# Another order for the weight splits of a Strassen-Winograd expert layer

## The chip, the cores and the metric

The kernel runs on one core of one Trainium2 chip. The metric is the device time of one execution in microseconds (us). Engines are named as the profile names them: PE is TensorE, DVE is VectorE, ACT is ScalarE, POOL is GpSimd, SP is the queue from which this kernel issues its loads and stores.

## The reference, cut to what matters

Causal attention with a forgetting bias (4 batches, 8 heads, 576 positions, head size 64) gives an array x of 2304 x 512. It goes through a mixture of four dense experts:

```python
p = domain_probs / (domain_probs.sum(-1, keepdims=True) + 1e-09)
out = np.zeros((N, D), dtype=np.float32)
for e in range(E):                       # E = 4, D = 512, F = 1024
    h = np.maximum(x @ w1[e], 0.0)
    out += p[:, e:e + 1] * (h @ w2[e])
```

The change lies in the experts' part alone, in the way in which w2 is made ready.

## The kernel before, in words

Every float32 operand of a matmul is split into a high and a low half in a rounded format (suffixes h and l: `w1h`, `w1l`, `w2h`, `w2l`), and each product is taken as high x high, high x low and low x high. A split is two steps: `hi` (L371) writes the rounded copy, here always on ACT, and `sub` (L366, instruction on L367) takes the copy from the original, on DVE or POOL.

Up to about 418 us the kernel computes attention and expert 0, interleaved by a planner. Then comes the Strassen part: experts 1 to 3, each cut into two halves of its hidden columns (`HALVES`, six of them, n = 0 to 5), each half over three groups of 768 rows (`PAIRS`, g = 0 to 2). That makes 18 pieces of work. For one piece the first layer and the second layer are each a 2 x 2 block product done with seven products instead of eight. The first layer (`first_layer`, matmuls on L1044) takes its products in the order 1, 6, 5, 7, 2, 4, 3, twelve matmuls of 384 columns each. The second (`second_layer`, L1052) takes them in the order 4, 1, 2, 6, 5, 7, 3, eighteen matmuls of 256 columns each, six into each of three PSUM banks.

The six PSUM banks of `pb` and the two of `mo` are handed on as follows. First layer: products 1, 6, 7 and 4 add up in the pair `bA`, products 5 and 3 in `bB`, product 2 in `bC`. Between them ACT copies `bA` out (`keep`, L1082, two activations, called c11, c12, c22 and h21) and DVE adds `bB` or `bC` to such a copy (`plus`, L1086, two instructions, called c22, c11 and c12). Second layer: product 4 writes `lB`, which is both banks of `bC` and then the second bank of `bB`; product 1 writes `lA`, which is the two `mo` banks and the first of `bB`. DVE then adds the result to `acc` (`update`, L1145).

The loop runs the first layer of the next piece ahead of the second layer of the present one, so PE goes L1(0), L1(1), L2(0), L1(2), L2(1) and so on. Everything else is laid by hand into the gaps between products: behind each first-layer product o, `after(o)` issues the load of the next operand (SP), then the steps of the table `at` for o, and then steps of the list `side` (two of them in the very first piece, one in all others).

- The table steps make the second layer's activation operands. In most pieces the table is `REST = {1: "6 5", 6: "s3 7", 5: "3"}`: behind product 6 step s3 (a DVE instruction, L1056, that reads the copy c12) and then operand 7 (high half on ACT into `xg`, low half on POOL), behind product 5 operand 3 (high half on ACT into `hx`, which reads the result of s3, low half on POOL). In the very first piece the table is `START = {7: "4", 2: "1", 4: "s5 s7"}`.
- `side` holds, when a new half's w2 is due, the seven splits that `w_steps(2)` returns. In the first piece (n = 0) that is L1(0); for n = 1 to 5 it is the first layer of piece (n, 1), the last one before the second layer of (n, 0) needs the new w2. Each split is `hi` on ACT into `w2h` and `sub` on DVE into `w2l`. Two POOL sums (L849) hang on them: behind split 5, source 6 is made from source 5, in the same buffer `t`; behind split 2, source 4 is made from source 6 and the buffer `w2r` that split 2 has read. So split 6 waits for the first sum, and split 4 for the second.

Each engine works its own queue strictly in the order in which these functions issue; semaphores order the engines among themselves.

Of the kernel before, what the change touches and what calls it, by code (L numbers as in the profile page):

```python
# [277 lines left out]
def body(ctx, tc, qk, vp, s, dp, w1, w1s, w2, w2s, out):  # L278
# [87 lines left out]
    def sub(e, out, in0, in1):  # L366
        (nc.gpsimd if e == "POOL" else nc.vector).tensor_tensor(out=out, in0=in0, in1=in1, op=ALU.subtract)  # L367
# [10 lines left out]
    def hi(e, out, in_):  # L378
        if e == "ACT":
            nc.scalar.activation(out, in_, AF.Copy)  # L380
        elif e == "POOL":
            nc.gpsimd.tensor_scalar(out, in_, 1.0, 1.0, op0=ALU.mult, op1=ALU.mult)
        else:
            nc.vector.tensor_copy(out, in_)
# [76 lines left out]
    for j, (h, ms) in enumerate(VISITS):  # L461
        base = 1000.0 * (j + 1)
        b, hh = divmod(h, NH)
        o = 64 * (hh % 2)
# [34 lines left out]
        else:  # L499
            if pq:  # L500
                qk_ready = [ld, ldc]
            else:
# [6 lines left out]
                def f(e, j=j, h=h, ext=ext):  # L509
                    nc.sync.dma_start(out=tok["KK", j][0:64, :, 0:ext].bitcast(F32), in_=AB(j)[64:128, 0:1, 0:ext].bitcast(F32).to_broadcast([64, 2, ext]))  # L510
                    nc.sync.dma_start(out=tok["KK", j][64:128, 0, 0:ext].bitcast(F32), in_=AB(j)[64:128, 1, 0:ext].bitcast(F32))
                    nc.sync.dma_start(out=tok["KK", j][64:68, 1, 0:ext].bitcast(F32), in_=ced[h, 2:6, 0:ext])
# [250 lines left out]
    for gi, tiles in enumerate(GROUPS0):  # L763
# [4 lines left out]
        else:  # L768
# [9 lines left out]
            at = max(i for i, x in enumerate(prog) if x[0] == "l1e") + 1  # L778
# [50 lines left out]
    def temp():  # L829
        return tpool.tile([P, 2, TG], F32, tag="t", name="t")  # L830
# [9 lines left out]
    def load_operand(g, o):  # L840
        t = x_tile()
        if o in BASE:
            load_block(t, g, *BASE[o])
        else:
            nc.sync.dma_start(out=flat4(t), in_=xsv[g, SUMS[o]])
        return t

    def add(e, out, in0, in1, op):
        (nc.gpsimd if e == "POOL" else nc.vector).tensor_tensor(out=out, in0=in0, in1=in1, op=op)  # L849
# [69 lines left out]
    def w_steps(which, begin=False):  # L919

        b = stage.pop(which)
        neg = which == 2
        part = w1_part if which == 1 else w2_part
        src = {1: b[0, 0], 2: b[1, 0], 3: b[1, 1], 7: b[0, 1], 4: b[1, 0]}

        def sums():
            if begin:
                src[5], src[6], src[4] = (t.rearrange("p a b -> p (a b)") for t in (spool.tile([P, 1, 512], F32, tag="t2", name="t2"), temp(), temp()))
                src[5], src[6], src[4] = (t[:, 0:512] for t in (src[5], src[6], src[4]))
                add("POOL", src[5], b[0, 1], b[0, 0], ALU.subtract)  # L930
                add("POOL", src[7], b[1, 1], b[0, 1], ALU.subtract)
                add("POOL", src[6], b[1, 1], src[5], ALU.subtract)
                add("POOL", src[4], b[1, 0], src[6], ALU.subtract)
                return
            src[5] = src[6] = spool.tile([P, 1, 512], F32, tag="t2", name="t2")[:, 0]
            add("POOL", src[5], b[0, 1], b[0, 0], ALU.subtract)
            add("POOL", src[7], b[1, 1], b[0, 1], ALU.subtract)

        def split(o, e):
            hi("ACT", part(o, 0), src[o])  # L940
            sub(e, part(o, 1), src[o], part(o, 0).bitcast(F32))
            if begin:
                pass
            elif o == 5 and neg:
                add("POOL", src[6], src[5], b[1, 1], ALU.subtract)
            elif o == 5:
                add("POOL", src[6], b[1, 1], src[5], ALU.subtract)
            if o == 2 and not begin:
                add("POOL", src[4], src[4], src[6], ALU.add if neg else ALU.subtract)

        return [sums] + [lambda o=o, e=e: split(o, e) for o, e in (
            tuple((o, "DVE") for o in PRODUCTS) if begin else
            ((5, "POOL"), (1, "POOL"), (2, "POOL"), (6, "POOL"), (4, "POOL"), (7, "DVE"), (3, "DVE")) if which == 1 else
            ((5, "DVE"), (2, "DVE"), (1, "DVE"), (7, "DVE"), (6, "DVE"), (4, "DVE"), (3, "DVE")))]

    pmoe = ctx.enter_context(tc.tile_pool(name="psm", bufs=1, space=PSUM))
    pb = [pmoe.tile([P, 512], F32, name=f"pb{i}") for i in range(6)]
# [20 lines left out]
    def w1_sums():  # L978
        w1_first.extend(w_steps(1, True))
        w1_first.pop(0)()  # L980
# [58 lines left out]
    def product(o, x, ts, start):  # L1039
        wv = [w1_part(o, l).rearrange("p (k f) -> p k f", k=2) for l in range(2)]  # L1040
        for u in range(2):
            for k in range(2):
                for n, (wl, xl_) in enumerate(((0, 0), (0, 1), (1, 0))):
                    nc.tensor.matmul(ts[u][:, 0:TG], wv[wl][:, k, 128 * u:128 * u + 128], x[:, xl_, k, :],  # L1044
                                     start=start and k == 0 and n == 0, stop=k == 1 and n == 2, skip_group_check=not start)
# [18 lines left out]
    side = []  # L1064

    def first_layer(w_i, at, tmp):

        nxt = work[w_i + 1] if w_i + 1 < len(work) else None

        def after(o):  # L1070
            if nxt is not None:
                xt[o] = load_operand(nxt[1], o)
            for f in at.get(o, ()):
                f()
            for _ in range(1 if w_i else 2):
                if side:
                    side.pop(0)()

        def keep(name, ts, f=AF.Copy):
            tmp[name] = temp()  # L1080
            for u in range(2):
                nc.scalar.activation(tmp[name][:, u], ts[u][:, 0:TG], f)  # L1082

        def plus(name, ts):
            for u in range(2):
                nc.vector.tensor_tensor(out=tmp[name][:, u], in0=ts[u][:, 0:TG], in1=tmp[name][:, u], op=ALU.add)  # L1086

        product(1, xt[1], bA, True)
        keep("c11", bA)
        after(1)  # L1090
        product(6, xt[6], bA, False)
        keep("c12", bA)
        after(6)
        product(5, xt[5], bB, True)
        after(5)
        product(7, xt[7], bA, False)
        keep("c22", bA)
        plus("c22", bB)
        after(7)
        product(2, xt[2], bC, True)  # L1100
        plus("c11", bC)
        after(2)
        product(4, xt[4], bA, False)
        keep("h21", bA, AF.Relu)
        after(4)
        product(3, xt[3], bB, False)
        plus("c12", bB)
        after(3)
# [26 lines left out]
    def plan(steps, table):  # L1135
        return {o: [steps[x] for x in names.split()] for o, names in table.items()}

    def second_layer(n, g, at):
# [44 lines left out]
        after(3)  # L1183

    side.extend(w_steps(2))
    tmp = {}
    steps = operands(tmp)
    first_layer(0, plan(steps, START), tmp)
    for w_i, (n, g) in enumerate(work):
        more = n + 1 < len(HALVES)  # L1190
        if w_i + 1 < len(work):
            if g == 0 and more:
                stage_w1(*HALVES[n + 1])
            if g == 1 and more:
                w1_next = w_steps(1)
                side.append(w1_next.pop(0))
                stage_w2(*HALVES[n + 1])
            if g == 0 and n:
                side.extend(w2_next)
            tmp = {}  # L1200
            at = plan(steps, REST if w_i else FIRST)
            steps = operands(tmp, w_i + 2 == len(work))
            if w_i + 2 == len(work):
                at.update(plan(steps, LAST))
            first_layer(w_i + 1, at, tmp)
            while side:
                side.pop(0)()
        if g == 1 and more:
            side.extend(w1_next)
        if g == 2 and more:  # L1210
            w2_next = w_steps(2)
            side.append(w2_next.pop(0))
        second_layer(n, g, plan(steps, EARLY if w_i + 2 < len(work) else ALL if w_i + 2 == len(work) else {}))
        while side:
            side.pop(0)()
# [29 lines left out]
```

## Time and profile before

| | us |
|---|---|
| timed runs | 971.43, 969.35, 965.13; median 969.35 |
| the profiled execution, its own time | 966.64 |
| its span, first to last instruction | 964.9 |
| PE busy within the span | 944.0 (98%) |
| mean granted TensorE clock, as a share of full speed | 0.989 |

The profile records one execution. Its span is 1.7 us shorter than the time of the same execution, which is what lies around the first and the last instruction. A timeline row gives the start, the duration, engine, line, operation, the tile written and the tiles read, and in brackets the idle time of the engine ahead of it with what ended it; an "x2" row is two instructions back to back, and its duration covers both. An instruction's record begins when it leaves its engine's queue, so a wait for a resource inside the engine lengthens the record and is not shown as idle time.

### The profile page before, as it was taken

What the parts mean: (1) busy time and instruction counts of PE and PEld (TensorE: products, weight loads), DVE (VectorE), ACT (ScalarE), POOL (GpSimd) and SP (SyncE); (2) the same over time, 40 slices, a digit from 0 to 9 for tenths busy, and PEclk for the clock granted to TensorE, in tenths of its full rate; (3) what the DMA queues carried; (4) which work ended last, traced back from release to release, by engine and by line L of the source; (5) the groups of instructions that cost most, each with busy time, mean ns of one, the idle gap of its engine ahead of it and who ended that gap; (6) DMA issues with size and microseconds to landing.
All of it is one profiled execution on the core that took longest, in us unless ns stands there. A gap on an engine that the chain in (4) does not pass through costs nothing.

```text
span 964.9 us, 18367 instructions
## 1 busy us (share of the span) xinstructions
PE 944.0 (98%) x6346; PEld 891.5 (92%) x6346; DVE 734.5 (76%) x1825; ACT 446.7 (46%) x1144; POOL 450.0 (47%) x505
## 2 busy tenths in 40 slices
PE   9989999999999999999999999999999999999998
PEld 6668889898898999999999999999999999999998
DVE  5879889889886222257688967997797979688976
ACT  4658787777775211244343344423343425343341
POOL 4456555655541389522381265317343624481222
PEclk7989999999999999999999999999999999999999
DMA  5857766757642596759645666555865468644613
GB/s 144 223 148 195 207 187 194 212 168 211 172 138 92 190 336 242 267 170 373 218 147 200 219 229 221 190 179 187 273 231 168 156 221 273 224 146 152 217 34 115
DMA packets 125975, 189.75 MB, mean 197 GB/s; under 512 B 10478, under 2 KB 102154, under 8 KB 125882
## 3 DMA queue, kind: packets, MB, share of 16 engines
q1 hardware_dynamic: 125882, 188.57, 61.0%
q8 instruction: 51, 0.84, 0.3%
q14 instruction: 42, 0.34, 0.1%
HBM read 144.73 MB, written 29.54 MB: 181 GB/s over the span
## 4 chain that ended last, share of the span: by engine, by line
PE 80%; DVE 11%; ACT 2%; DMA 2%; issue 2%; POOL 2%; DVEq 0%; SPq 0%; ACTq 0%; POOLq 0%
PE pb L1052 20%; PE pb L1044 19%; PE mo L1052 8%; PE mo L759 6%; PE mo L746 5%; PE T L599 5%; DVE w2l L367 4%; PE pv L658 4%; PE pb L746 4%; PE pb L759 3%; PE S L551 3%; PE S L545 2%; DMA x<-x_d 1%; DVE t L1086 1%; DVE a L562 1%
## 5 line engine op out<-in xcount | busy, mean ns | idle before, releaser
L1044 PE MATMUL pb<-x,w1h 128*128 128x384 f32 x1008 | 255.9, 334 | 0.5 <-ACT t L1082 0.5
L1044 PEld LDWEIGHTS pb<-x,w1h 128*128 128x128 f32 x1008 | 181.2, 188 | 0.9 <-ACT t L1082 0.8
L1044 PE MATMUL pb<-x,w1l 128*128 128x384 f32 x504 | 168.4, 334 | 0.0
L367 POOL TENSOR_TENSOR hT_r<-t,hT_r 128x768 fp32r<-128x768 f32 x18 | 33.9, 1885 | 273.8 <-ACT hT_r L380 177.4
L1082 ACT ACTIVATE t<-pb 128x384 f32<-128x384 f32 x144 | 67.0, 487 | 169.4 <-PE pb L1044 160.2
L1145 DVE SCALAR_TENSOR_TENSOR acc<-pb,prob,acc 128x256 f32<-128x256 f32 x288 | 126.2, 474 | 9.4 <-PE pb L1052 9.2
L375 POOL TENSOR_SCALAR a<-a,sm 64x64 f32<-64x64 f32 (+4 forms) x147 | 92.0, 630 | 67.2 <-DVE sm L578 39.6
L1052 PE MATMUL pb<-w2h,hT_r 128*128 128x256 f32 x720 | 115.7, 283 | 0.1
L570 ACT ACTIVATE a<-a,mx 64x64 f32<-64x64 f32 (+4 forms) x160 | 89.6, 562 | 26.9 <-DVE mx L562 16.5
L1052 PEld LDWEIGHTS pb<-w2h,hT_r 128*128 128x128 f32 x720 | 100.0, 191 | 0.5 <-DVE t L1086 0.3
L1059 ACT ACTIVATE hT_r<-t 128x768 fp32r<-128x768 f32 x54 | 45.7, 846 | 108.1 <-PE pb L1052 104.5
L1044 PEld LDWEIGHTS pb<-x,w1l 128*128 128x128 f32 x504 | 94.6, 188 | 0.0
L1086 DVE TENSOR_TENSOR t<-pb,t 128x384 f32<-128x384 f32 x108 | 56.2, 550 | 50.3 <-PE pb L1044 35.1
L1056 DVE SCALAR_TENSOR_TENSOR t<-t 128x768 f32<-128x768 f32 x72 | 88.0, 1223 | 2.2 <-ACT t L1082 2.1
L746 PE MATMUL mo<-xg,w1h 128*128 128x256 f32 (+1 forms) x344 | 80.5, 308 | 1.0 <-DVE xg L367 1.0
L599 PE MATMUL T<-idn,a 128*128 128x128 f32 x473 | 74.9, 281 | 6.7 <-POOL a L375 3.6
L380 ACT ACTIVATE aTh<-T 128x256 fp32r<-128x256 f32 (+2 forms) x278 | 65.6, 308 | 28.3 <-PE T L599 23.9
L1052 PE MATMUL pb<-w2l,hT_r 128*128 128x256 f32 x360 | 73.0, 284 | 5.1 <-DVE w2l L367 5.1
L635 DVE TENSOR_TENSOR aTl<-T,aTh 128x64 fp32r<-128x64 f32 (+3 forms) x247 | 72.6, 334 | 6.3 <-ACT aTh L380 5.2
L599 PEld LDWEIGHTS T<-idn,a 128*128 128x128 f32 x473 | 55.0, 143 | 21.1 <-issue 7.1
L562 DVE CUSTOM_DVE_ANT_0 a<-S,mask 128x192 f32<-128x192 f32 (+4 forms) x151 | 61.9, 419 | 3.9 <-PE S L545 1.9
L1145 DVE SCALAR_TENSOR_TENSOR acc<-mo,prob,acc 128x256 f32<-128x256 f32 x144 | 62.7, 474 | 1.6 <-PE mo L1052 1.6
(160 smaller groups left out, 2101.7 us busy)
## 6 DMA issues: line engine op xcount, KB each, us to landing
x<-xs_d SPq DMA_DIRECT2D x68, 768.0 KB
x<-x_d SPq DMA_DIRECT2D x55, 768.0 KB
xs_d<-x SPq DMA_DIRECT2D x12, 768.0 KB
raw<-in_qk_dram SPq DMA_DIRECT2D x24, 288.0 KB
KK<-AB_r SPq DMA_DIRECT2D x24, 288.0 KB
x_d<-xh SPq DMA_DIRECT2D x12, 576.0 KB
w1r<-in_w1s_dram SPq DMA_DIRECT2D x6, 1024.0 KB
w2r<-in_w2s_dram SPq DMA_DIRECT2D x6, 1024.0 KB
```

The source lines that it names most:

```text
L367: (nc.gpsimd if e == "POOL" else nc.vector).tensor_tensor(out=out, in0=in0, in1=in1, op=ALU.subtract)
L375: (nc.gpsimd if e == "POOL" else nc.vector).tensor_scalar(out, in_, scale, 1.0 if bias is None else bias, op0=ALU.mult, op1=ALU.mult if bi ...
L562: nc.vector.tensor_tensor_reduce(out=z[0:n, j0:j1], in0=tok["S", (c, pi)][0:n, 0:j1 - j0], in1=mask[0:n, 448 - a + j0:448 - a + j1], scale ...
L570: nc.scalar.activation(z[0:n, 0:bb], z[0:n, 0:bb], AF.Exp, bias=tok["mx", c][0:n, k:k + 1], scale=-1.0, accum_out=tok["sm", c][0:n])
L599: nc.tensor.transpose(t[:, 128 * k:128 * k + 128], z[:, 128 * x:128 * x + 128], idn)
L635: nc.vector.tensor_tensor(out=dst, in0=src, in1=h_.bitcast(F32), op=ALU.subtract)
L746: nc.tensor.matmul(t[:, 0:w], wl[q][:, dc, o:o + P], xgt[:, l, dc, 0:w], start=(u == 0), stop=(u == 3 * KD - 1))
L759: nc.tensor.matmul(t, ht[:, fc, 128 * ti:128 * ti + 128], wl[fc // 2][:, fc % 2, :], start=(u == 0), stop=(u == 3 * KF - 1))
L1044: nc.tensor.matmul(ts[u][:, 0:TG], wv[wl][:, k, 128 * u:128 * u + 128], x[:, xl_, k, :], start=start and k == 0 and n == 0, stop=k == 1 an ...
L1052: nc.tensor.matmul(ts[t][:, 0:256], h_part(o, hl_)[:, k, 128 * t:128 * t + 128], wv[wl][:, k, :], start=start and k == 0 and n == 0, stop= ...
L1056: (nc.gpsimd if e == "POOL" else nc.vector).scalar_tensor_tensor(out=out, in0=in0, scalar=0.0, in1=in1, op0=ALU.max, op1=op)
L1145: nc.vector.scalar_tensor_tensor(out=a_, in0=ts[t][:, 0:256], scalar=prob[:, tt, e:e + 1], in1=a_, op0=ALU.mult, op1=ALU.add)
```

## The change

Two edits. The order in which `w_steps(2)` hands out the seven splits of w2 goes from 5, 2, 1, 7, 6, 4, 3 to 5, 2, 6, 4, 1, 7, 3. And behind first-layer product 6 the side steps are issued ahead of the table's steps; behind all other products they stay behind them.

```diff
             ((5, "POOL"), (1, "POOL"), (2, "POOL"), (6, "POOL"), (4, "POOL"), (7, "DVE"), (3, "DVE")) if which == 1 else
-            ((5, "DVE"), (2, "DVE"), (1, "DVE"), (7, "DVE"), (6, "DVE"), (4, "DVE"), (3, "DVE")))]
+            ((5, "DVE"), (2, "DVE"), (6, "DVE"), (4, "DVE"), (1, "DVE"), (7, "DVE"), (3, "DVE")))]
...
         def after(o):
             if nxt is not None:
                 xt[o] = load_operand(nxt[1], o)
-            for f in at.get(o, ()):
+            steps_ = at.get(o, ())
+            splits = [side.pop(0) for _ in range(1 if w_i else 2) if side]
+            for f in (*splits, *steps_) if o == 6 else (*steps_, *splits):
                 f()
-            for _ in range(1 if w_i else 2):
-                if side:
-                    side.pop(0)()
```

The splits of w1 and the steps of the second layer are handed out as before.

## Rows read from the trace of the kernel before

**Rows 1.** The page, part 1: busy time, share of the span, instructions

```profile
PE 944.0 (98%) x6346; PEld 891.5 (92%) x6346; DVE 734.5 (76%) x1825; ACT 446.7 (46%) x1144; POOL 450.0 (47%) x505
```

**Rows 2.** PE's waits over the span, the longest sum: us in total, times, longest

```profile
PE pb L1052 <- DVE w2l L367: 5.1, 5, 1.0
```

**Rows 3.** Stretches, one piece each: length, busy PE, PEld, DVE, ACT, POOL, clock

```profile
493.26:522.93 29.67, 29.67 (x211) 29.67 (x211) 24.00 (x44) 9.18 (x15) 9.57 (x6) 1.00 0.65 221
522.93:553.88 30.95, 29.94 (x212) 29.73 (x211) 28.74 (x47) 12.70 (x22) 10.04 (x5) 1.00 0.64 214
```

**Rows 4.** The chain that ended last: one first layer without waits (start, us)

```profile
553.88 14.56 PE pb L1044 x84
```

**Rows 5.** Timeline of PE, 537.2 to 540.9: the second layer's first product

```profile
537.34 0.63 PE L1052 MATMUL pb<-w2h,hT_r 128*128 128x256 f32 x4
538.98 0.50 PE L1052 MATMUL pb<-w2l,hT_r 128*128 128x256 f32 x2 [1.01 <-DVE w2l L367]
539.32 0.64 PE L1052 MATMUL pb<-w2h,hT_r 128*128 128x256 f32 x4
...
540.04 0.64 PE L1052 MATMUL pb<-w2h,hT_r 128*128 128x256 f32 x4
```

**Rows 6.** Timeline of DVE, 529 to 540, ahead of the same second layer

```profile
529.46 0.94 DVE L1056 SCALAR_TENSOR_TENSOR t<-t 128x768 f32<-128x768 f32 x1
530.33 4.04 DVE L367 TENSOR_TENSOR w2l<-w2r,w2h 128x512 fp32r<-128x512 f32 x2
...
535.22 0.85 DVE L367 TENSOR_TENSOR w2l<-w2r,w2h 128x512 fp32r<-128x512 f32 x1
535.99 1.01 DVE L1086 TENSOR_TENSOR t<-pb,t 128x384 f32<-128x384 f32 x2
536.92 1.40 DVE L367 TENSOR_TENSOR w2l<-t,w2h 128x512 fp32r<-128x512 f32 x1
538.25 0.68 DVE L367 TENSOR_TENSOR w2l<-w2r,w2h 128x512 fp32r<-128x512 f32 x1
538.85 1.01 DVE L1086 TENSOR_TENSOR t<-pb,t 128x384 f32<-128x384 f32 x2
```

**Rows 7.** Timeline of ACT, 528 to 537

```profile
528.17 0.86 ACT L380 ACTIVATE xg<-t 128x768 fp32r<-128x768 f32 x1
...
530.43 0.85 ACT L380 ACTIVATE hx<-t 128x768 fp32r<-128x768 f32 x1 [0.89 <-DVE t L1056]
...
531.71 0.85 ACT L1082 ACTIVATE t<-pb 128x384 f32<-128x384 f32 x2
...
535.84 1.15 ACT L380 ACTIVATE w2h<-w2r 128x512 fp32r<-128x512 f32 x2
```

**Rows 8.** Timeline of POOL, 529 to 538

```profile
529.61 1.95 POOL L849 TENSOR_TENSOR t<-t,w2r 128x512 f32<-128x512 f32 x1 [0.63 <-DVE w2l L367]
531.52 2.29 POOL L367 TENSOR_TENSOR xg<-t,xg 128x768 fp32r<-128x768 f32 x1
533.77 1.75 POOL L849 TENSOR_TENSOR w2r<-w2r,t 128x512 f32<-128x512 f32 x1
535.48 2.29 POOL L367 TENSOR_TENSOR hx<-t,hx 128x768 fp32r<-128x768 f32 x1
```

**Rows 9.** Timelines of DVE and of POOL around 442

```profile
441.52 2.60 DVE L1056 SCALAR_TENSOR_TENSOR t<-t 128x768 f32<-128x768 f32 x1
441.42 1.88 POOL L367 TENSOR_TENSOR hT_r<-t,hT_r 128x768 fp32r<-128x768 f32 x1 [15.18 <-ACT hT_r L380]
```

**Rows 10.** Timelines of POOL, DVE, ACT and PE in the first piece, 424 to 434

```profile
424.63 1.61 POOL L849 TENSOR_TENSOR w2r<-w2r,t 128x512 f32<-128x512 f32 x1 [0.85 <-DVE w2l L367]
427.31 1.01 DVE L1086 TENSOR_TENSOR t<-pb,t 128x384 f32<-128x384 f32 x2
433.11 0.85 ACT L1082 ACTIVATE t<-pb 128x384 f32<-128x384 f32 x2
433.64 0.62 PE L1044 MATMUL pb<-x,w1h 128*128 128x384 f32 x2 [0.52 <-ACT t L1082]
```

## The prediction

> **What bounds the kernel now.** I read the busy times first. PE is busy for 944.0 of 964.9 us [rows 1], so only PE's gaps can be won back, and whatever makes a new gap is paid in full. Next came PE's waits. In the Strassen part there are five waits for `w2l`, 5.1 us together and the longest 1.0, so all about equal [rows 2], and one of 0.52 us for the copy `t` in the first piece [rows 10]. The stretches then tell where the five lie: a piece without a wait lasts 29.67 us, the piece in which a new w2 is split lasts 30.95 [rows 3], so each wait costs 1.28 us, a little more than its idle time (the first matmuls behind a wait run slower: six that take 0.72 us elsewhere took 1.98 around the wait [rows 5]). As the five are equal, one piece worked out in detail holds for all. The ceiling of the change is therefore 5 x 1.28 = 6.4 us, with 0.8 more if the wait of the first piece went.
>
> In the timelines of this piece PE reaches the first `w2l` matmul of product 4 at 537.8 and gets it at 538.98, right behind split 4 on DVE, which ran from 538.25 to 538.93 [rows 5, 6]. The question is whether DVE's queue is merely in a bad order or simply late. Two things say late. Behind split 4 stands `plus` c12, 538.85 to 539.86 [rows 6], and it frees the bank that PE's third tile wants at 540.04 [rows 5]: with split 4 out of the way PE would find this bank ready only 0.1 us before today's time. And DVE's records are stretched: a split that takes 0.68 us at 538.25 takes 1.40 at 536.92, and two take 4.04 at 530.33 [rows 6].
>
> **What stretches them.** The ends line up with POOL's. Split 6 ends at 538.32, 0.55 behind POOL's end at 537.77; the pair ends at 534.37, 0.56 behind POOL's end at 533.81 [rows 6, 8]. The other way round POOL's first sum, begun at 529.61 while s3 was running, ends at 531.56, 1.16 behind the end of s3 at 530.40 [rows 6, 8]. Step s3's form waits too: at 441.52 it lasted 2.60 instead of 0.94 and ended 0.82 behind POOL [rows 6, 9]. `plus`, which reads one operand from PSUM, took 1.01 for two beside POOL's step of 535.48 (the pair at 535.99) and 1.01 without it (538.85) [rows 6, 8]. So a DVE and a POOL instruction that each read two SBUF tiles run one after the other, and when both queues are full they take turns. I use these figures: DVE split 0.68 alone, 0.55 behind POOL; s3 0.82 behind POOL; POOL's 512-column sum 1.16 behind DVE, its 768-column step 1.88 alone and 1.70 behind DVE (537.77 less the 536.07 at which the split of 535.22 ended) [rows 6, 8, 9].
>
> The Trainium skill (SBUF — State Buffer, "Who interferes with whom") says that issue order decides which of the two blocks for a whole instruction; the rows above agree. It makes the order of issue the thing to replay, and by it alone a reordering at equal work could come out either way.
>
> **The change, step by step, in the piece at 522.77.** It adds and removes no instruction and no DMA; SP's loads are issued ahead of both kinds of step, as before. Seven splits still stand on DVE, six of them ahead of `plus` c12. What changes is who meets whom, so I write the queues out anew from 529.46, the point at which split 5 has just ended and `after(6)` begins.
>
> 1. DVE now begins with split 2: 529.46 to 530.14. POOL's first sum, released at 529.61, follows it: to 530.14 + 1.16 = 531.30 (was 531.56).
> 2. s3 is now behind split 2 and meets that sum: it waits to 531.30 and ends at 532.12 (was 530.40). 1.7 us lost.
> 3. POOL's second sum, now ahead of operand 7, ends at 532.12 + 1.15 = 533.27 (was 535.52). This is what the change does for split 4.
> 4. ACT stands at operand 3's high half, which reads s3: 532.15 to 533.00 (was 530.43 [rows 7]). Behind it in ACT's queue are the high half of split 6 (0.62, half of 1.15 for two [rows 7]), to 533.52, and `keep` c22, whose two copies now end at 533.9 and 534.3 (was 531.71 to 532.56 [rows 7]).
> 5. PE: a product takes 14.56 / 7 = 2.08 us [rows 4], so with the second layer at 537.34 product 4 was due at 533.18. It adds into the bank that `keep` c22 reads, and now waits to 533.96: 0.78 idle, about 0.9 with the slow first matmuls. A new wait.
> 6. DVE's split 6 is ready at 533.55, but POOL has taken the turn at 533.27 with operand 7 and holds it to 535.15. Split 6 ends at 535.70, `plus` c22 at 536.6. POOL's operand 3 ends at 535.70 + 1.70 = 537.40, split 4 at 537.95, `plus` c11 at 538.9, split 1 at 539.5, split 7 at 540.1, `plus` c12 at 541.0 (was 539.86).
> 7. PE, 0.9 late, starts the second layer at 538.3 to 538.4. Split 4 is there (537.95), so the old wait is gone; but the third tile's bank comes free at 541.0 instead of 539.86, and PE begins it at 541.05 and runs its first matmuls 0.1 slower. Against 540.04 that is 1.1 us later.
>
> The same replay with the old order gives split 4 at 538.9 and the third tile at 540.1, as in the trace. The net is +1.1 us in each of five pieces, +5.5. Bounds: DVE could end no later than before, with PE then waiting for `plus` c12 at 539.9 (-0.1 a piece); at the other end one more 768-column step of POOL could fall in front of `plus` c12, of which half again is likely to be hidden (+1.9 a piece). I take 1.1, since 1.16, 0.55, 0.82 and 1.70 each come from rows with the same two instructions.
>
> **The first piece.** Here two splits stand behind each product; the new order puts 2 and 6 behind product 6, 4 and 1 behind product 5. Split 4's high half must wait for POOL's second sum, which ended at 426.24 [rows 10], and ACT has `keep` c22 behind it. So ACT: 426.3, two high halves (1.15 [rows 7]) to 427.4, first copy at 427.9; `plus` c22 starts at 428.2, not at 427.31 [rows 10]. Everything behind it on DVE and ACT is a closed chain up to `keep` h21 at 433.11, which releases PE at 433.64 [rows 10]: this chain, and so PE, slips by 0.86. PE's product 4 (due near 428.8, two products before 433) still finds its bank free. Bounds 0 and 1.2; I take 0.9.
>
> **The sum.** 5 x 1.1 + 0.9 = 6.4 us, on the profiled execution's 966.64: 973.0. That execution is 2.7 below the median of the three runs; all four together have their middle at 968.0 (halfway between 966.64 and 969.35). I put the change on that: 968.0 + 6.4 = 974.4 us, slower by 0.7%.
>
> **The rivals.**
> - *Faster: the wait simply goes.* Split 4 is ready 1 us earlier in step 6, and the wait for `w2l` is the only one that the profile names. It decides if DVE, too, gets through `plus` c12 at least 1.3 us sooner, so that all of 539.86 moves below 538.7. Price: -6.4, 961.6 us. Against it: `plus` c12 has as many splits ahead as before, and the turns with POOL are the same in number. The Trainium skill (Perfetto Trace Analysis, "Optimization Strategy") advises to find what PE's gap waits for and make that start sooner, which would give this time; the row of `plus` c12, 0.2 us ahead of PE [rows 5, 6], speaks against it here. Chance 0.10.
> - *No change: another wait takes its place at the same spot.* If DVE catches up in step 6 (split 6 taking its turn ahead of operand 7; 0.28 us decide), `plus` c12 ends near where it did: five times -0.1 to +0.4, and 0 to 0.9 in the first piece, 968 to 971. Chance 0.17.
> - *Worse:* the late `plus` c22 also delays product 3's bank, and an extra step of POOL falls ahead of `plus` c12: five times 1.9 and 1.2, 979 us. Chance 0.08.
>
> **How the numbers follow.** The forecast has 0.65. Its own range is 0.7 to 1.5 a piece and 0 to 1.2 in the first piece, 971.5 to 976.7, and with the 3 us by which the runs of before lie on either side of their middle 969 to 980. The range to hold the time 8 times in 10 takes in the no-change case and most of the worse one: 965 to 981. A measurement of this kernel can tell about 1% from no change, 9.7 us. The forecast and the no-change case lie within it, the faster rival too, unless the runs help it (0.02 over 1%); the worse case and the upper end of the forecast pass it with 0.12.
>
> **What would show it.** In the changed kernel PE's waits should hold no `w2l` any more, but five of about 0.8 us for `t` of ACT (product 4) and five of about 1.0 for `t` of DVE (third tile), and the first piece's 0.5 should have become 1.4; the piece of 30.95 should last 32.1. s3 should run for 2.0 us in a split piece. If the piece is shorter than 30.95, or s3 ends ahead of POOL's first sum, steps 2 to 7 are wrong.

## The result, and the profile after

The changed kernel takes 975.76 us (median of six runs, 973.75 to 979.28); the kernel before has 968.78 over six, the three runs of the table above among them. The ratio is 1.0083 with a 95% interval of 1.0054 to 1.0112: slower, by a little under 1%. The forecast was 974.4 us, slower by 0.7%.

Where the time went is read from stretches. This view of the changed kernel has one piece of work per row: length, busy time of PE, weight loads, DVE, ACT, POOL, clock.

```profile
499.49:529.16 29.67, 29.67 (x212) 29.67 (x211) 24.02 (x44) 9.19 (x15) 9.74 (x6) 1.00 0.65 221
529.16:561.13 31.97, 30.55 (x213) 29.62 (x211) 28.36 (x46) 12.69 (x22) 9.49 (x5) 1.00 0.62 207
```

A piece without splits is what it was, 29.67. A piece in which w2 is split went from 30.95 [rows 3] to 31.97, with PE idle for 1.42 us of it. The waits of PE over the whole span (us, times, longest) name two holders; five waits of each lie in the split pieces, and the sixth of the first row in the first piece:

```profile
PE pb L1044 <- ACT t L1081: 4.4, 6, 1.4
PE pb L1052 <- DVE t L1085: 4.2, 5, 0.8
```

The entry for `w2l` [rows 2] is gone; line numbers are one lower than before. The timeline of PE places the two in the split piece that began at 529.16:

```profile
540.32 0.62 PE L1044 MATMUL pb<-x,w1h 128*128 128x384 f32 x2 [0.58 <-ACT t L1081]
547.35 0.74 PE L1052 MATMUL pb<-w2h,hT_r 128*128 128x256 f32 x4 [0.84 <-DVE t L1085]
```

The first is product 4 of the first layer, waiting for the copy c22. The second is the third tile of the second layer's product 4, waiting for the addition c12. This piece began 6.39 us later on the clock than the one at 522.77, so 547.35 stands for 540.96 there, against 540.04 [rows 5]: 0.9 later. The timeline of DVE shows why; it answers to [rows 6]:

```profile
535.85 0.68 DVE L367 TENSOR_TENSOR w2l<-w2r,w2h 128x512 fp32r<-128x512 f32 x1
536.45 2.04 DVE L1056 SCALAR_TENSOR_TENSOR t<-t 128x768 f32<-128x768 f32 x1
539.92 2.05 DVE L367 TENSOR_TENSOR w2l<-t,w2h 128x512 fp32r<-128x512 f32 x1 [1.43 <-ACT w2h L380]
...
542.83 1.40 DVE L367 TENSOR_TENSOR w2l<-w2r,w2h 128x512 fp32r<-128x512 f32 x1
...
546.29 1.01 DVE L1085 TENSOR_TENSOR t<-pb,t 128x384 f32<-128x384 f32 x2
```

Split 2 runs alone in 0.68. Step s3 behind it takes 2.04 instead of 0.94, DVE then stands idle for 1.43 until ACT has the high half of split 6, and that split takes 2.05. The partners are in the timelines of POOL and of ACT ([rows 8] and [rows 7] before):

```profile
536.00 1.67 POOL L849 TENSOR_TENSOR t<-t,w2r 128x512 f32<-128x512 f32 x1 [0.63 <-DVE w2l L367]
537.75 1.89 POOL L849 TENSOR_TENSOR w2r<-w2r,t 128x512 f32<-128x512 f32 x1
539.60 1.82 POOL L367 TENSOR_TENSOR xg<-t,xg 128x768 fp32r<-128x768 f32 x1
541.38 2.31 POOL L367 TENSOR_TENSOR hx<-t,hx 128x768 fp32r<-128x768 f32 x1
```

```profile
538.52 0.85 ACT L380 ACTIVATE hx<-t 128x768 fp32r<-128x768 f32 x1 [2.58 <-DVE t L1056]
539.27 0.62 ACT L380 ACTIVATE w2h<-t 128x512 fp32r<-128x512 f32 x1
539.79 0.85 ACT L1081 ACTIVATE t<-pb 128x384 f32<-128x384 f32 x2
```

Step s3 ends at 538.49, 0.81 behind POOL's first sum (537.67); split 6 ends at 541.97, 0.55 behind operand 7 (541.42). ACT waits 2.58 for s3 with the high half of operand 3, and behind it in ACT's queue stand split 6 and the copy c22.

Five split pieces of 31.97 to 31.99 instead of 30.95 to 30.97 make 5.1 us. The first two pieces together take 45.97 instead of 45.06, 0.9 more; there the wait for the copy h21 grew from 0.52 [rows 10] to 1.44. From the start of the Strassen part to the end of the span that is 552.50 us instead of 546.50, and these 6.0 us are all that the change does. The profiled execution itself took 978.13, 11.5 more than the one before; the other 5.5 lie ahead of the first changed instruction, where both kernels issue the same work (last section).

### The profile page after: what moved, and what is told of

Read it like the earlier page. It is cut to its first block, busy times and chain, and to the rows that moved or that the text cites. A ratio compares the mean times of both kernels' runs of the same rounds, so it can differ in the third digit from the quotient of the medians.

```text
span 976.4 us, 18372 instructions
## 1 busy us (share of the span) xinstructions
PE 952.1 (98%) x6346; PEld 894.7 (92%) x6346; DVE 730.7 (75%) x1825; ACT 447.3 (46%) x1144; POOL 446.2 (46%) x505
## 4 chain that ended last, share of the span: by engine, by line
PE 75%; DVE 12%; DMA 4%; ACT 3%; issue 3%; POOL 1%; SPq 0%; DVEq 0%; ACTq 0%; POOLq 0%
PE pb L1044 19%; PE pb L1052 19%; PE mo L1052 8%; PE mo L759 6%; PE mo L746 4%; PE T L599 4%; PE pb L746 3%; PE pb L759 3%; PE pv L658 3%; DVE w2l L367 3%; PE S L551 3%; DVE t L1085 2%; DVE aTl L635 1%; DVE a L562 1%; DMA x<-x_d 1%
## 5 line engine op out<-in xcount | busy, mean ns | idle before, releaser
L1056 DVE SCALAR_TENSOR_TENSOR t<-t 128x768 f32<-128x768 f32 x72 | 93.5, 1298 | 2.2 <-ACT t L1081 2.1
L551 PE MATMUL S<-KK,AB_r 128*128 128x288 f32 (+9 forms) x288 | 62.1, 315 | 2.1 <-DVE mx L562 1.7
```

Of the source, the lines that this page charges most:

```text
L551: nc.tensor.matmul(t[:, 0:j1 - j0], AB(j)[0:k, x, a:a + P], tok["KK", j][0:k, x, j0:j1], start=(x == 0), stop=(x == 1))
L1056: (nc.gpsimd if e == "POOL" else nc.vector).scalar_tensor_tensor(out=out, in0=in0, scalar=0.0, in1=in1, op0=ALU.max, op1=op)
```

## The experiments

The lengths of like pieces repeat within 0.03 us inside one execution, so they tell theories apart that whole times could not. Theory A is the one of the prediction: DVE and POOL take turns, and POOL's steps are what makes DVE late. Theory B says that only the order in the queues matters and POOL runs beside DVE for nothing.

**The two edits one at a time.** First the order of the splits alone:

```diff
-            ((5, "DVE"), (2, "DVE"), (1, "DVE"), (7, "DVE"), (6, "DVE"), (4, "DVE"), (3, "DVE")))]
+            ((5, "DVE"), (2, "DVE"), (6, "DVE"), (4, "DVE"), (1, "DVE"), (7, "DVE"), (3, "DVE")))]
```

> The new order of the splits alone; behind product 6 the table's steps stay first. Measured by the length of a split piece (from the start of its first layer to that of the next one; 30.95 us before, 31.98 after) and of the first two pieces together (45.06 before, 45.97 after). Theory A, taking turns: DVE and POOL instructions that each read two SBUF tiles run one after the other, and the piece is as long as DVE's queue is late at its last additions. Split 4 must now wait on DVE for POOL's second sum, which still stands behind operand 7, so the additions c11 and c12 are as late as with the whole change: 32.1 us, with no wait at product 4, about 1.2 us for t of DVE ahead of the second layer and about 1.0 at its third bank. First two pieces 45.97. Theory B, queue order alone: what the change costs is that ACT's copy c22 stands behind operand 3 and s3; without the step ahead the copy is on time again, split 4 is early, and the piece is 29.7 us, at most 30.95.

Measured: 31.98 to 31.99 a split piece, first two pieces 45.99. PE's waits in one split piece, with the DVE row that bears on the first of them:

```profile
539.15 0.71 PE L1052 MATMUL pb<-w2h,hT_r 128*128 128x256 f32 x4 [0.98 <-ACT w2h L380]
541.66 0.74 PE L1052 MATMUL pb<-w2h,hT_r 128*128 128x256 f32 x4 [0.84 <-DVE t L1086]
```

```profile
538.46 1.01 DVE L1086 TENSOR_TENSOR t<-pb,t 128x384 f32<-128x384 f32 x2
```

The sums over the span:

```profile
PE pb L1052 <- DVE t L1086: 7.1, 8, 1.0
PE pb L1052 <- ACT w2h L380: 2.0, 2, 1.0
```

The length is that of A, and no wait stands at product 4. Ahead of the second layer PE waits 0.97 to 0.98 in each split piece. The view puts two of these five waits down to a high half on ACT and the other three to DVE's addition c11. In the piece shown ACT had made the high half of split 4 by 537.37, while the first of the two additions of c11 ended at 539.01, 0.14 ahead of PE's start; so here too the addition is what PE waits for, as A has it.

Then the step ahead alone, with the old order of the splits:

```diff
-            for f in at.get(o, ()):
+            steps_ = at.get(o, ())
+            splits = [side.pop(0) for _ in range(1 if w_i else 2) if side]
+            for f in (*splits, *steps_) if o == 6 else (*steps_, *splits):
                 f()
-            for _ in range(1 if w_i else 2):
-                if side:
-                    side.pop(0)()
```

> The other edit alone: the split ahead of the table's steps behind product 6, the splits in the old order. Theory A: split piece 32.1 us; PE waits 0.6 us for the copy t of ACT at product 4 and about 1.1 us for w2l in the second layer's first product, since DVE is as late as with the whole change. First two pieces 45.06 as before, because nothing stands in the table behind product 6 there. Theory B: the new wait at product 4 lies ahead of the old one for w2l, which shrinks by as much: 31 us.

Measured: 32.0 a split piece, first two pieces 45.07. The waits of a split piece:

```profile
531.48 0.61 PE L1044 MATMUL pb<-x,w1h 128*128 128x384 f32 x2 [0.58 <-ACT t L1081]
537.58 0.51 PE L1052 MATMUL pb<-w2l,hT_r 128*128 128x256 f32 x2 [0.86 <-DVE w2l L367]
```

Either edit by itself costs the five pieces as much as both together, about 1.0 us each, by different waits. The costs don't add, since both work through the same lateness of DVE: counted from the start of the piece and put on the time scale of the kernel before, the addition c12 ends at 540.93 with the order alone, at 540.91 with the step ahead alone and at 540.91 with both (539.86 before). And the 0.9 us of the first piece belong to the order alone.

**POOL's steps taken away.** The low halves of operands 7 and 3 are left out in the split pieces, once in the changed kernel and once in the kernel before:

```diff
     def operand(o, t, e):
         hi("ACT", h_part(o, 0), t)
+        if bare[0] and o in (7, 3):
+            return
         sub(e, h_part(o, 1), t, h_part(o, 0).bitcast(F32))
...
+            bare[0] = g == 0 and n > 0
             first_layer(w_i + 1, at, tmp)
+            bare[0] = False
```

> The changed kernel, in the five split pieces without POOL's low halves of operands 7 and 3 (left out: the second layer then takes stale low halves of these two). Theory A: DVE is held up by neither, split 6 ends at 1.4 us and the addition c12 at 1.9 us earlier than with the change; only the wait at product 4 stays, which comes from s3 behind POOL's first sum: 30.6 us a split piece, no wait for t of DVE. Theory B: POOL's steps run beside DVE and cost it nothing: 32.0 us.

> The kernel before with the same left out: in the five split pieces no low halves of operands 7 and 3 on POOL. Theory A: split 4 ends some 1.7 us earlier, at the time PE reaches product 4 of the second layer, and the wait for w2l goes: 29.67 us a split piece, the length of a piece without splits. Theory B: 30.95 us.

Measured: 30.53 to 30.56 in the changed kernel, and 29.67 in the kernel before, in all five pieces. PE's waits of the changed kernel without the two steps hold no `t` of DVE any more:

```profile
PE pb L1044 <- ACT t L1081: 4.4, 6, 1.4
```

DVE's timeline there, from split 2 to split 4:

```profile
530.45 0.68 DVE L367 TENSOR_TENSOR w2l<-w2r,w2h 128x512 fp32r<-128x512 f32 x1
531.05 2.04 DVE L1056 SCALAR_TENSOR_TENSOR t<-t 128x768 f32<-128x768 f32 x1
534.52 0.69 DVE L367 TENSOR_TENSOR w2l<-t,w2h 128x512 fp32r<-128x512 f32 x1 [1.43 <-ACT w2h L380]
535.13 1.01 DVE L1085 TENSOR_TENSOR t<-pb,t 128x384 f32<-128x384 f32 x2
536.07 0.68 DVE L367 TENSOR_TENSOR w2l<-w2r,w2h 128x512 fp32r<-128x512 f32 x1
```

In the kernel before without the two steps, splits 2 and 1 take 2.38 together instead of 4.04 [rows 6]:

```profile
529.84 2.38 DVE L367 TENSOR_TENSOR w2l<-w2r,w2h 128x512 fp32r<-128x512 f32 x2
```

In the changed kernel the same split 6 that took 2.05 takes 0.69 when POOL has nothing for it to meet, while s3, whose partner (the first sum) is still there, keeps its 2.04. Theory B falls with these two runs. They also show that the wait for `w2l` in the kernel before was POOL's doing: split 4 stood in its old, late place in the queue and the wait was gone.

**The step ahead made harmless at one point.** In the changed kernel operand 3 goes behind product 7:

```diff
-            at = plan(steps, REST if w_i else FIRST)
+            at = plan(steps, ({**REST, 5: "", 7: "3"} if g == 0 else REST) if w_i else FIRST)
```

> The changed kernel with operand 3 (high half on ACT, low half on POOL) moved from behind product 5 to behind product 7 in the split pieces. This takes s3 out of the way of ACT's copy c22, and puts POOL's step for operand 3 behind the next split. Theory A, taking turns: the wait at product 4 goes, split 6 takes its turn ahead of both POOL steps, but operand 3's step still falls ahead of the last additions: c12 as late as in the kernel before, one wait of about 1.2 us at the third bank, 31.0 us a split piece. If only the copy c22 mattered: 31.98 less 0.7, 31.3, and if the order of the splits were all that kept it from the length without splits: 29.67.

Measured: 30.91 a split piece, with one wait left in the timeline of PE:

```profile
543.83 0.74 PE L1052 MATMUL pb<-w2h,hT_r 128*128 128x256 f32 x4 [0.98 <-DVE t L1085]
```

That is the third bank, as A has it. So even with split 4 early and the copy c22 on time, the reordering ends where the kernel before stood, because the addition c12 is as late as it was: on the time scale of the kernel before it ends at 539.86, as there.

**What beats both: moving POOL's steps, not the splits.** The kernel before, old order of splits, with operands 7 and 3 behind the last product of the split pieces:

```diff
-            at = plan(steps, REST if w_i else FIRST)
+            at = plan(steps, ({1: "6 5", 6: "s3", 3: "7 3"} if g == 0 else REST) if w_i else FIRST)
```

> The kernel before with the splits in the old order; only the steps of operands 7 and 3 are moved, in the five split pieces, to behind product 3, so that POOL takes them when DVE has its splits behind it. Nothing is left out. Theory A: POOL's two steps no longer take turns with splits 1, 7 and 6; split 4 is ready when PE wants it and c12 ends at 538.2 instead of 539.9 on the time scale of the kernel before: 29.67 us a split piece, no wait for w2l, first two pieces unchanged 45.06; 5 x 1.28 = 6.4 us faster than before (0.7%). Theory B (the order of the splits sets it): 30.95, no gain.

Measured: 29.67 in every piece, first two 45.07; 960.09 us (median of four; the kernel before beside it 966.75), ratio 0.9935, interval 0.9919 to 0.9950. Since nothing is left out, missing work can't be the reason. Its timelines of DVE and of POOL show the turns that are no longer taken:

```profile
530.16 2.38 DVE L367 TENSOR_TENSOR w2l<-w2r,w2h 128x512 fp32r<-128x512 f32 x2
...
535.10 0.68 DVE L367 TENSOR_TENSOR w2l<-t,w2h 128x512 fp32r<-128x512 f32 x1
536.34 0.69 DVE L367 TENSOR_TENSOR w2l<-w2r,w2h 128x512 fp32r<-128x512 f32 x1 [0.56 <-ACT w2h L380]
536.95 1.01 DVE L1086 TENSOR_TENSOR t<-pb,t 128x384 f32<-128x384 f32 x2
538.32 1.20 DVE L367 TENSOR_TENSOR w2l<-w2r,w2h 128x512 fp32r<-128x512 f32 x1 [0.36 <-ACT w2h L380]
```

```profile
532.08 1.61 POOL L849 TENSOR_TENSOR w2r<-w2r,t 128x512 f32<-128x512 f32 x1 [0.69 <-DVE w2l L367]
537.12 1.85 POOL L367 TENSOR_TENSOR xg<-t,xg 128x768 fp32r<-128x768 f32 x1 [3.42 <-ACT xg L380]
538.92 2.31 POOL L367 TENSOR_TENSOR hx<-t,hx 128x768 fp32r<-128x768 f32 x1
```

Splits 2 and 1, 4.04 together before [rows 6], take 2.38, and split 6 takes 0.68 instead of 1.40. DVE then stands idle ahead of split 4, so it is no longer late, and c12 ends 1.74 sooner than in the kernel before, counted from the start of the piece. POOL takes operands 7 and 3 when DVE has only split 3 of the seven left, which takes 1.20 for it; the products that read these operands, and split 3, are the sixth and seventh of the second layer.

**The first piece.** Two tries to win its 0.8 us too. First the new order with POOL's steps late, without the step ahead behind product 6, and in the first piece one entry of `side` behind each product; against the kernel before, this last edit is:

```diff
-            for _ in range(1 if w_i else 2):
+            for _ in range(1):
```

> The new order of the splits, operands 7 and 3 behind product 3 in the split pieces, and in the first piece one split behind each product instead of two. Nothing is left out. Theory A: 29.67 us a split piece, and in the first piece the copies c22 and h21 are no longer held up, so that the first two pieces take 29.67 + 14.56 = 44.2 us instead of 45.06: 5 x 1.28 + 0.8 = 7.2 us faster than before (0.7%), about 14 us faster than the changed kernel. Theory B: 30.95 or more a split piece, and within 1 us of the kernel before.

Measured: 29.73 a split piece, but 45.17 for the first two; 960.64 us (median of six), ratio 0.9943 (0.9924 to 0.9962). With POOL's steps out of the way the order of the splits thus matters by 0.06 us a piece (29.73 against 29.67). The size for the first piece was a miss. In the very first piece the list `side` begins with the two sums on POOL from which the splits start, so that with one entry behind each product split 5 falls behind product 6, split 4 behind product 2, and split 3 into the next piece. ACT's timeline at the end of the first piece, and PE's in the second:

```profile
432.21 0.85 ACT L1059 ACTIVATE hT_r<-t 128x768 fp32r<-128x768 f32 x1 [2.04 <-DVE t L1086]
432.96 0.62 ACT L380 ACTIVATE w2h<-w2r 128x512 fp32r<-128x512 f32 x1
433.48 0.85 ACT L1082 ACTIVATE t<-pb 128x384 f32<-128x384 f32 x2
```

```profile
434.00 0.61 PE L1044 MATMUL pb<-x,w1h 128*128 128x384 f32 x2
...
444.94 0.62 PE L1044 MATMUL pb<-x,w1h 128*128 128x384 f32 x2 [0.26 <-ACT t L1082]
```

The split behind product 2 puts its high half right ahead of the copy h21, so that PE still loses 0.39 at 434.00 (0.80 in the kernel before). It then loses another 0.53 at product 4 of the second piece, 444.94, which waits for the copy c22 there. Counted from the start of the first piece, this copy begins 0.28 later than in the kernel before, while PE comes sooner; splits 1 and 7 on DVE now stand in the second piece ahead of what leads to it, but that they are the reason was not tried alone. The last try takes the old order, POOL's steps late, and keeps splits 4 and 3 of the first piece behind the copy h21:

```diff
-            for _ in range(1 if w_i else 2):
+            for _ in range(1 if w_i else {7: 0, 2: 0, 4: 1, 3: 1}.get(o, 2)):
```

> The kernel before with operands 7 and 3 behind product 3 in the split pieces, and in the first piece splits 4 and 3 moved from behind product 7 to behind products 4 and 3, behind the copy h21 on ACT. Nothing is left out. Theory A: 29.67 us a split piece; in the first piece DVE reaches the addition c11 1.2 us earlier, the copy h21 is made before PE wants its bank, and the first two pieces take 44.2 us instead of 45.06. Together 5 x 1.28 + 0.8 = 7.2 us faster than before (0.7%). If the first piece has another holder of h21, its two pieces stay near 45 and the gain is 6.4 us.

Measured: 29.67 in all fifteen pieces behind the first two, and 44.30 for these two. The stretch of these two has PE busy throughout:

```profile
418.80:463.10 44.30, 44.30 (x296) 44.21 (x295) 34.95 (x56) 19.13 (x33) 9.10 (x5) 1.00 0.86 297
```

The time is 960.42 us (median of six), ratio 0.9934, interval 0.9915 to 0.9953. From the start of the Strassen part to the end it takes 539.23 us, 7.3 less than the kernel before and 13.3 less than the changed one. Against the run with only POOL's steps moved (539.99) the 0.8 us are seen in the stretch; whole times don't resolve them.

## Why the prediction was right

- **What bounds the kernel.** That PE waits for `w2l`, but that DVE is late rather than badly ordered, held. Split 4 came early and the time was lost all the same at c12 in the changed kernel and in the run with operand 3 moved, and at c11 and c12 with the order alone.
- **Taking turns.** The figures carried over: s3 0.81 behind POOL (0.82 was used), splits 0.55, POOL's sum 1.15 behind DVE (537.67 less 536.52). The Trainium skill (SBUF — State Buffer, "Who interferes with whom") has the later of the two block fully until the first is done; the 0.69 against 2.05 of the same split agrees. That the two then alternate is this trace's own: at 537.67 s3 goes next although POOL has another sum in its queue.
- **Steps 1 to 7.** Shifted by 6.39 us, split 2 ended at 530.13 (530.14 forecast), s3 at 532.10 (532.12), POOL's second sum at 533.25 (533.27), split 6 at 535.58 (535.70), c12 at 540.91 (541.0). The third tile began at 540.96 (541.05). Two slips in the working did no harm. Step 4 calls 0.62 the half of 1.15, but 0.62 is what one high half takes alone, and 1.15 holds two that overlap; the step adds 0.52, which the trace bears out. And PE came to the second layer at 538.46, not at 538.3 to 538.4: its first matmuls of product 3 and the start of the second layer lost another 0.10 and 0.14 us. That stays hidden, because c12 ends later still.
- **A term slightly off.** 1.1 us a piece was forecast, 1.0 measured (31.98 less 30.96). The 0.1 is in step 6: operand 7 on POOL was done 0.12 sooner than put there (541.42 less 6.39 is 535.03, not 535.15), and c12 with it. The idle times shown, 0.58 and 0.84, are below the 0.78 and 1.0 named, because the view counts a gap only from the modelled end of the matmul ahead.
- **The first piece.** 0.9 forecast, 0.91 measured, with the wait for h21 at 1.44 (1.4 forecast).
- **The sum.** 6.4 forecast, 6.0 measured in the Strassen part. The medians differ by 7.0 (975.76 less 968.78), whose interval, 5.2 to 10.9 us from the ratio's, holds both; what the medians show beyond 6.0 is no more than the start of the kernel varies by (last section).
- **The rivals.** "The wait simply goes" named a time, 961.6, that the kernel does reach or pass (960.1 to 960.6 in three versions), but by another edit than this one: moving POOL's steps. Starting split 4 alone sooner, by reordering, gave nothing (30.91 at best); with POOL's steps moved it is done 1.74 sooner, c12 with it, and the wait is gone. The Trainium skill (Perfetto Trace Analysis, "Optimization Strategy") advises to make what is waited for start sooner or complete faster; these runs agree once one asks what makes it late. "No change" failed at the 0.28 us named: POOL had taken the turn for operand 7 at 539.60 to 539.64, and DVE asked for it at 539.92.

## What to carry to other kernels

Before reordering what an engine waits for, look at the lengths of equal instructions: one form that took 0.68 in one place and 2.05 in another had a partner here, and the ends of its records told which. Then move the partner: the same two POOL steps, placed where DVE is not on PE's path, were worth 6.4 us, while reordering DVE's own queue cost 6.0. And look one instruction behind the one that PE waits for; here that was late too, and the wait only changed its name.

## What was not expected

The part ahead of the Strassen part, in which the changed kernel and the kernel before issue the same instructions, ended at 423.85 us in the profile of the changed kernel and at 418.36 in that of the kernel before. In the eight other profiles it ended between 415.90 and 421.39. The difference lies mostly in the first 100 us. The stretch of the kernel before, then that of the changed kernel:

```profile
0.00:100.00 100.00, 92.75 (x532) 73.34 (x533) 78.37 (x317) 62.60 (x213) 52.66 (x95) 0.90 0.65 177
```

```profile
0.00:100.00 100.00, 93.97 (x502) 73.32 (x502) 72.31 (x296) 58.37 (x196) 49.71 (x90) 0.95 0.62 169
```

PE got through 502 matmuls instead of 532, though its granted clock was higher (0.95 against 0.90) and it was as busy. What holds it back there was not tried and stays open. Equal stretches of the Strassen part agree from profile to profile (45.06 to 45.08 in the four profiles in which the first two pieces were left alone, 29.67 for every piece without splits). So this start is likely why runs of one kernel differ by 6 us (965.13 to 971.43 for the kernel before), but that isn't shown, because each kernel has one profile. It is why this change is better read from its stretches than from two whole times.
